# Sixteen weight transfers moved to another engine's queue, and every step ordered anew, in a fused attention and feed-forward kernel

## The chip, the cores and the metric

The kernel runs on one core of a Trainium2 chip. Its time is the device time in microseconds (us) of one execution; of several runs the median is given. Before the change three runs took 532.25, 532.66 and 536.98 us, so the median is 532.66 us.

## The reference: what is computed

Inputs r, k, v, w are (4 batches, 8 heads, 768 positions, 48), u is (8, 48), all as 64-bit floats; w_in is 384 x 2048 and w_out is 2048 x 384. A recurrent attention runs over the positions, and its output goes through a feed-forward stage:

```python
for t in range(S):
    cur = einsum('bhd,bhe->bhde', u * k[t], v[t])
    y[t] = einsum('bhd,bhde->bhe', r[t], state + cur)
    state = w[t][..., None] * state + einsum('bhd,bhe->bhde', k[t], v[t])
x = y.transpose(0, 2, 1, 3).reshape(B * S, H * D)      # 3072 x 384
h = maximum(x @ w_in, 0.0)
out = (h * h) @ w_out
```

## The kernel before, in words

**Tiles.** The 768 positions are cut into 6 chunks of 128. For each chunk and each of the 4 batches (a unit; 24 in all) the attention is done in matrix form, and its result x is written as a high and a low part. When the batches of a chunk have their x, the feed-forward stage takes them: w_in and w_out are held as 8 groups, each of two 128-wide blocks f, so there are 16 steps f for each chunk. A step is nine matmuls into a PSUM bank `hp` (line 852), relu on ScalarE (L857), square (ScalarE L859 in chunk 0, VectorE L861 later), a rounded high part on ScalarE (L863), the rest on VectorE (L864), and then three matmuls for each batch into that batch's bank `ob` (L870). A step takes all four batches (512 columns, "full width") or, by `HALF`, only two (256 columns): the first 6 steps of chunk 0 and all 16 of chunk 1 are done in halves.

**Weights.** The weights arrive as 64-bit numbers. `load_w` fetches a group of w_in by five transfers into `ri` (L398: one to 96 partitions, two to 48 and two to 16) and a group of w_out by one into `ro` (L400), all issued on SP. `split_w` makes high and low parts of each: a widening copy on ScalarE (L411), three integer operations on VectorE (L415, L419, L424), a cast on ScalarE (L431) and a subtraction on GpSimd (L432). The result is `wi` and `wo`, which L852 and L870 read.

**Attention.** In chunk 0 TensorE turns the inputs (L496), VectorE scans the decay (L508), ScalarE and VectorE form its logarithms and quotients (L515 to L535), TensorE forms bonus terms (L548), scores (L736) and outputs (L760, L777, L752, L770). From chunk 1 on the turned inputs `pt` come by transposes on VectorE (L460) and transfers inside SBUF (L470), and the matmuls are L608, L626 (outer products), L653 (scores), L644 (state times r) and L663 (output). Pieces of x are copied between partitions by transfers issued on SP (L705).

**Order.** Every piece of work is a step that `P.add` records with its engine and the steps it depends on. The table `ORDER` then says in which order all 2473 steps are issued; as each engine runs its own instructions in order, the table fixes the queue of every engine. `PLACES` says which buffer of a pool each use gets. `FILLS` puts filler matmuls (L334: transposes of the identity matrix into an unused part of PSUM, no result is read) ahead of some TensorE steps; 16 more run at the start. The steps of `load_w` are made in a loop:

```python
for i, (to, src) in enumerate(pieces):
    n = (2 * R, D, D, D, D)[i]
    P.add("sp", (1.45, 0.72, 0.72, 0.47, 0.47)[i], rank(0), lambda to=to, src=src: nc.sync.dma_start(out=to, in_=src),
          w=[("wi", g, i)], after=before, runs=n, issue=0.48)
```

The functions that the change touches:

Of the kernel before, what the change touches and what calls it, by code (L numbers as in the profile page):

```python
# [96 lines left out]
class Names:  # L97
# [122 lines left out]
def kernel(  # L220
# [11 lines left out]
    nc = tc.nc  # L232
# [3 lines left out]
    DM, DF = w_in.shape  # L236
    C = 128
# [4 lines left out]
    HP = J + D  # L242
# [772 lines left out]
```

## Time and profile before

| | |
|---|---|
| median of three runs | 532.66 us |
| span of the profiled execution | 533.0 us |
| TensorE busy (matmul) | 515.3 us, 97% |
| VectorE busy | 358.4 us, 67% |
| ScalarE busy | 312.6 us, 59% |
| granted TensorE clock, mean | 0.999 |
| filler matmuls | 142, 22.7 us of TensorE's busy time |

The span reaches from the first to the last instruction; no other time of the profiled execution is given, so the span is what the sum is made against. It lies 0.3 us above the median. A busy engine is not one that does useful work: fillers count as busy, and a matmul's end is modelled. Idle time of an engine matters only where another waits for it.

### The profile page before, as it was taken

The page shows a single profiled execution, that of the slowest core. Times are in us where ns is not written, and L with a number is a line of the kernel's source. Part 1 is how long each engine was busy: PE and PEld are TensorE (multiplying, and loading weights), DVE is VectorE, ACT ScalarE, POOL GpSimd, SP SyncE. Part 2 cuts the span into 40 slices and gives each one's busy share as a digit, 9 for nine tenths or more (in the row PEclk, how much of TensorE's full clock was granted, in tenths as well). Part 3 has the DMA queues.
Part 4 walks back from the last instruction along what each step waited for, and adds up shares of the span by engine and source line. Part 5 has one row for each costly group of instructions (what it writes and reads, how often), then busy time and mean ns, then how long its engine had stood idle before and what let it go on. Part 6 is the DMA issues. An engine that isn't in the chain of part 4 may idle for free.

```text
span 533.0 us, 13849 instructions
## 1 busy us (share of the span) xinstructions
PE 515.3 (97%) x5478; PEld 464.7 (87%) x5478; DVE 358.4 (67%) x782; ACT 312.6 (59%) x858; POOL 77.6 (15%) x117
## 2 busy tenths in 40 slices
PE   8998999999999999899999999999999999999996
PEld 8787998778899989788998988898998898989995
DVE  4899887887768799766877768648366654333332
ACT  2778888777675667757557384655345554432322
POOL 2012441242403030030300300201200000000000
PEclk9999999999999999999999999999999999999999
DMA  9999869946465655636555363543450010200001
GB/s 144 168 241 218 179 148 204 236 81 119 85 129 121 117 117 109 124 77 129 107 92 110 61 134 73 100 77 80 89 117 1 5 31 17 71 6 1 0 1 63
DMA packets 222982, 53.07 MB, mean 100 GB/s; under 512 B 212672, under 2 KB 217792, under 8 KB 222912
## 3 DMA queue, kind: packets, MB, share of 16 engines
q1 hardware_dynamic: 222192, 51.15, 48.1%
q8 instruction: 45, 0.74, 0.6%
q10 hardware_dynamic: 720, 0.98, 0.6%
q14 instruction: 25, 0.20, 0.1%
HBM read 31.65 MB, written 4.72 MB: 68 GB/s over the span
## 4 chain that ended last, share of the span: by engine, by line
PE 69%; SPq 3%; DVE 2%; DMA 2%; issue 0%; ACT 0%; POOL 0%; ACTq 0%; DVEq 0%; POOLq 0%
PE ob L870 31%; PE hp L852 30%; SPq L470 2%; PE ob L644 2%; PE ob L663 2%; PE a L653 2%; PE a L626 1%; PE hp L608 1%; DMA x<-x 1%; DVE st L460 0%; DMA pt<-st 0%; DMA v<-in_v_dram 0%; SPq L483 0%; PE hp L548 0%; DVE pt L508 0%
## 5 line engine op out<-in xcount | busy, mean ns | idle before, releaser
L870 PE MATMUL ob<-wo,g 128*128 128x384 f32 x1152 | 228.1, 341 | 2.1 <-ACT x L584 2.1
L852 PE MATMUL hp<-x,wi 128*128 128x512 f32 (+1 forms) x1062 | 220.9, 354 | 1.5 <-DVE g L864 1.3
L870 PEld LDWEIGHTS ob<-wo,g 128*128 128x128 f32 x1152 | 199.6, 188 | 9.6 <-ACT x L584 2.3
L852 PEld LDWEIGHTS hp<-x,wi 128*128 128x128 f32 x1062 | 174.6, 189 | 27.7 <-DVE g L864 4.0
L857 ACT ACTIVATE t<-hp 128x512 f32<-128x512 f32 (+1 forms) x118 | 61.0, 517 | 89.1 <-PE hp L852 53.5
L861 DVE SCALAR_TENSOR_TENSOR hp<-hp,t 128x512 f32<-128x512 f32 (+1 forms) x96 | 58.1, 605 | 78.3 <-ACT t L857 78.1
L864 DVE TENSOR_TENSOR g<-hp,g 128x512 fp32r<-128x512 f32 (+1 forms) x118 | 69.1, 586 | 39.9 <-ACT g L863 38.4
L863 ACT CAST g<-hp 128x512 fp32r<-128x512 f32 (+1 forms) x118 | 59.5, 507 | 47.0 <-DVE hp L861 46.2
L603 ACT ACTIVATE m<-diag,beta 128x64 f32<-128x64 f32 x160 | 40.3, 339 | 0.0
L508 DVE TENSOR_TENSOR_SCAN pt<-pt,zero 112x128 f32<-112x128 f32 x80 | 30.8, 420 | 7.3 <-DMA pt<-st 4.1
L634 POOL MEMSET S<- 1x1 f32 x16 | 1.4, 88 | 193.1 <-PE ob L644 192.5
L584 ACT ACTIVATE x<-ob 112x128 fp32r<-112x128 f32 x64 | 15.7, 277 | 21.0 <-PE ob L663 13.6
L557 POOL TENSOR_TENSOR st<-st 128x384 f32<-128x384 f32 x16 | 16.6, 1035 | 78.3 <-DVE st L460 53.2
L460 DVE STREAM_TRANSPOSE st<-st 128x1152 f32<-128x1152 f32 x20 | 26.9, 1360 | 0.2 <-DMA st<-in_w_dram 0.2
L587 DVE SCALAR_TENSOR_TENSOR x<-ob,x 112x128 fp32r<-112x128 f32 x64 | 16.6, 282 | 13.1 <-ACT x L584 9.3
L432 POOL TENSOR_TENSOR wi<-q,wi 128x768 fp32r<-128x768 f32 x8 | 16.2, 2026 | 50.1 <-ACT wi L431 46.5
L515 ACT ACTIVATE m<-pt 112x512 f32<-112x512 f32 x24 | 15.2, 632 | 9.0 <-DVE pt L508 8.8
L531 DVE TENSOR_TENSOR pt<-pt,m 112x512 f32<-112x512 f32 x24 | 17.2, 716 | 4.3 <-ACT Ec L530 1.9
L801 ACT COPY ob<-zero 112x128 f32<-112x128 f32 x64 | 16.3, 271 | 4.8 <-DVE x L587 3.2
L432 POOL TENSOR_TENSOR wo<-q,wo 128x768 fp32r<-128x768 f32 x8 | 14.8, 1856 | 25.0 <-ACT wo L431 22.7
L610 ACT COPY m<-hp 128x448 f32<-128x448 f32 (+1 forms) x20 | 9.9, 494 | 13.5 <-PE hp L608 13.2
L685 DVE COPY_PREDICATED m<-caus,a 128x256 f32<-128x256 uint8 x40 | 16.9, 439 | 1.1 <-PE a L653 1.0
(127 smaller groups left out, 540.1 us busy)
## 6 DMA issues: line engine op xcount, KB each, us to landing
pt<-st SPq DMA_DIRECT2D x120, 96.0 KB, 2.3
ro<-in_moe_w_out_dram SPq DMA_DIRECT2D x8, 768.0 KB, 6.6
v<-in_v_dram SPq DMA_DIRECT2D x96, 48.0 KB, 2.5
st<-in_r_dram SPq DMA_DIRECT2D x11, 384.0 KB, 5.1
st<-in_w_dram SPq DMA_DIRECT2D x11, 384.0 KB, 5.2
st<-in_k_dram SPq DMA_DIRECT2D x11, 384.0 KB, 4.6
out_dram<-q SPq DMA_DIRECT2D x20, 192.0 KB, 2.2
ri<-in_moe_w_in_dram SPq DMA_DIRECT2D x8, 384.0 KB, 5.2
```

The lines of the kernel that those rows point to most:

```text
L432: P.add("pool", 1.9, rank(8 * k + 5), lambda q=q, tt=tt: G.tensor_tensor(out=tt[:, 1], in0=q.tile, in1=tt[:, 0].bitcast(F32), op=ALU.subtr ...
L460: V.transpose(out=zt[:, i].rearrange("a t p q i -> a t (p q) i"), in_=sv[:, :, i].rearrange("s t p q x -> s t (p q) x"))
L508: lambda p=p: V.tensor_tensor_scan(out=pt[:, 0, p], data0=src(0)[:, p], data1=zero.broadcast_to([HP, C]), initial=1.0, op0=ALU.mult, op1=A ...
L531: P.add("dve", 0.6, rank("kn"), lambda: V.tensor_tensor(out=pt[:, 0], in0=pt[:, 0], in1=yv(), op=ALU.mult), r=[y0], w=EK, port=True)
L603: A.activation(M.tile[:, o:o + Q], diag2, AF.Copy, scale=beta.tile[:, i:i + 1])
L685: P.add("dve", 0.36, rank("mask"), lambda j=j: V.copy_predicated(out=mv(j), mask=caus[:, :, 0:Q].unsqueeze(1).broadcast_to([128, 2, 2, Q]) ...
L852: T.matmul(hp.tile[:, 0:n], wi[f][:, wl, kt], xT[:, kt, xl, xs], start=(m == 0), stop=(m == 3 * KT - 1))
L857: P.add("act", 0.49 if full else 0.28, rank("g1"), lambda: A.activation(t(), h(), AF.Relu), r=[hp], w=[(g, 1)])
L861: P.add("dve", 0.605 if full else 0.337, rank("g2"), lambda: V.scalar_tensor_tensor(out=h(), in0=h(), scalar=0.0, in1=t(), op0=ALU.max, op ...
L863: P.add("act", 0.48 if full else 0.26, rank("g3"), lambda: A.copy(out=hi(), in_=h()), r=[hp], w=[(g, 0)])
L864: P.add("dve", 0.605 if full else 0.335, rank("g4"), lambda: V.tensor_tensor(out=lo(), in0=h(), in1=hi().bitcast(F32), op=ALU.subtract), r ...
L870: T.matmul(obs[b][:, 0:DM], g.tile[0][:, gl, o:o + C], wo[f][:, wl], start=(f == 0 and m == 0), stop=(f == NF - 1 and m == 2))
```

## The change

Three things change in the code. The last two of the five transfers of each w_in group (the ones to 16 partitions, 16 transfers in all) are issued from ScalarE's queue; nothing is changed in what they move. `ORDER`, `PLACES` and `FILLS` are replaced throughout. The step that clears an output half of a PSUM bank (`clear`) gets a dependency on the chunk-0 steps that use this bank. Below, two lines of the tables stand for them.

```diff
 ORDER = (
-    0, 4, 11, 6, 94, 1, 14, 18, 5, 19, 20, 17, 10, 21, 8, 9, 139, 15, 7, 16, 12, 23, 2, 13, 24, 22, 25, 92, 26, 30, 27, 101,
...
+    2468, 2464, 2450, 2469, 2461, 2465, 2466, 2462, 2463, 2471, 2449, 2458, 2472, 2459, 2460,
 )
 FILLS = {
-    443: (2, 'a', 1), 571: (3, 'a', 0), 363: (3, 'a', 0), 370: (4, 'hp', 1), 578: (5, 'hp', 1), 493: (3, 'hp', 0), 645: (2, 'side', 0), 511: (6, 'side', 0),
-    520: (2, 'side', 0), 634: (5, 'side', 0), 663: (4, 'hp', 0), 1215: (1, 'hp', 1), 15: (29, 'ob', 1), 30: (8, 'ob', 3), 39: (6, 'ob', 0), 80: (6, 'ob', 2),
-    89: (5, 'hp', 0), 142: (3, 'hp', 0), 124: (12, 'ob', 0), 133: (11, 'ob', 0), 162: (6, 'ob', 0),
+    55: (4, 'ob', 0), 14: (3, 'ob', 0), 57: (6, 'ob', 1), 56: (6, 'ob', 1), 16: (9, 'ob', 1), 30: (8, 'a', 0), 140: (10, 'ob', 3), 39: (8, 'ob', 1),
+    41: (3, 'ob', 1), 48: (18, 'ob', 2), 100: (2, 'ob', 2), 80: (4, 'hp', 0), 82: (3, 'hp', 0), 89: (7, 'ob', 1), 121: (4, 'ob', 0), 124: (2, 'ob', 0),
+    126: (3, 'ob', 0), 167: (3, 'side', 0),
 }
...
         for i, (to, src) in enumerate(pieces):
             n = (2 * R, D, D, D, D)[i]
-            P.add("sp", (1.45, 0.72, 0.72, 0.47, 0.47)[i], rank(0), lambda to=to, src=src: nc.sync.dma_start(out=to, in_=src),
+            e = nc.sync if i < 3 else nc.scalar
+            P.add("sp" if i < 3 else "actq2", (1.45, 0.72, 0.72, 0.47, 0.47)[i], rank(0), lambda to=to, src=src, e=e: e.dma_start(out=to, in_=src),
                   w=[("wi", g, i)], after=before, runs=n, issue=0.48)
...
         for p in range(NP):
-            P.add("act", 0.16, rank("zero"), lambda p=p: A.copy(out=obs[p][0:HP, DM:], in_=zero[0:HP].broadcast_to([HP, C])), w=[("YO", p)], banks=1 << p)
+            turned = [s for s in P.steps if s.name.endswith(f" of chunk 0, batch {s.name[-1]}") and ("ob", p) in s.keys]
+            P.add("act", 0.16, rank("zero"), lambda p=p: A.copy(out=obs[p][0:HP, DM:], in_=zero[0:HP].broadcast_to([HP, C])), w=[("YO", p)], after=turned, banks=1 << p)
```

**What the order shows.** In the changed kernel, line numbers are 12 to 14 higher. The matmuls on TensorE are the same in number and shape, but for the fillers: 142 before, 119 now. Their places, counted in TensorE's queue between four marks that both orders have:

| stretch of TensorE's queue | fillers before | fillers now | other work that the order moves across the marks |
|---|---|---|---|
| up to the first half-width feed-forward step (L852, 128x256) | 73 | 107 | now also one more group of four L496 and one more of four L548 |
| from there to the first full-width step (group 3 of w_in) | 31 | 12 | that much less, and 57 matmuls L870 instead of 60 |
| from there to the first step of group 7 | 28 | 0 | 84 matmuls L870 instead of 81 |
| from there to the first full-width step of chunk 2 | 10 | 0 | the same |

The fillers of the first stretch include the 16 at the start. ScalarE's queue holds 5 of the 16 moved transfers ahead of the relu of the first half-width step, 8 more ahead of the relu of the first full-width step, and the last 3 behind it. A check of the decay values (one matmul, a comparison on VectorE and a read of the flag by every engine) moves from 472 us (L914) to the last steps of the program. Ahead of the latter relu it also holds one more cast of w_in, one of w_out (L431), one L578 and one L801 than before.

First place: TensorE's queue at the first half-width feed-forward step. `x_136` is x of chunk 0, `wi_57` group 0 of w_in, `st_138` raw inputs of batches 2 and 3, `ident` the identity. Before:

```order
L334 MATMUL hp_145<-ident 128x128 x3
L496 MATMUL a_147<-ident,st_138 128x128 x4
L852 MATMUL hp_146<-x_136,wi_57 128x256 x9
L548 MATMUL ob_141<-ut,m_161 128x4 x4
L496 MATMUL ob_143<-ident,st_138 128x128 x4
L852 MATMUL hp_145<-x_136,wi_57 128x256 x9
```

Now:

```order
L509 MATMUL ob_143<-ident,st_138 128x128 x4
L509 MATMUL a_148<-ident,st_138 128x128 x4
L866 MATMUL hp_145<-x_136,wi_57 128x256 x9
L866 MATMUL hp_146<-x_136,wi_57 128x256 x9
L346 MATMUL ob_141<-ident 128x128 x4
```

The bonus matmuls (L548) and the last turned inputs (L496) stood behind the first step and stand ahead of it now; the two blocks of group 0 follow each other.

Second place: ScalarE's queue between two widening copies of w_in and w_out (L411 before, L424 now). Before:

```order
L431 CAST wo_59<-q_150 128x768
L411 ACTIVATE q_149<-ri_60 128x768
L781 COPY ly_89<-a_147 112x128
L554 COPY beta_173<-ob_144 64x2x2x2 x2
L411 ACTIVATE q_150<-ro_62 128x768
L859 ACTIVATE hp_145<-t_96 128x256
```

Now, with `ri_60` group 1 and `ri_64` group 2 of raw w_in:

```order
L411 DMA ri_64<-in_moe_w_in_dram 16x3x512
L794 COPY ly_90<-a_147 112x128
L411 DMA ri_60<-in_moe_w_in_dram 16x3x512
L591 ACTIVATE st_137,far<-st_137,nfar 128x8x48
L529 ACTIVATE m_156<-m_156 112x512
L444 CAST wi_57<-q_150 128x768
L597 ACTIVATE x_136<-a_147 128x128
L597 ACTIVATE x_136<-a_148 128x2x128
L798 COPY m_158<-a_147 128x224
L798 COPY m_158<-a_148 128x224
L424 ACTIVATE q_149<-ri_60 128x768
```

The queue that evacuates PSUM now issues transfers too, and the copy that reads group 1 stands seven instructions behind the issue of that group's last piece. For group 2 there are six instructions between the two.

Third place: TensorE's queue in the first unit of chunk 1, between its outer products, its scores and the product with the state. Before:

```order
L626 MATMUL a_148<-v_153,m_158 48x48
L334 MATMUL hp_146<-ident 128x128 x4
L653 MATMUL a_147<-pt_129 64x64 x2
...
L334 MATMUL hp_146<-ident 128x128 x5
L644 MATMUL a_148<-pt_129,S_131 64x64
```

Now:

```order
L866 MATMUL hp_146<-x_136,wi_73 128x512 x9
L561 MATMUL hp_145<-ut,m_159 128x4 x4
L666 MATMUL a_147<-pt_129 64x64 x2
...
L884 MATMUL ob_141<-wo_75,g_99 128x384 x3
L884 MATMUL ob_144<-wo_71,g_97 128x384 x3
L884 MATMUL ob_144<-wo_75,g_99 128x384 x3
L884 MATMUL ob_142<-wo_71,g_97 128x384 x3
L657 MATMUL a_148<-pt_129,S_131 64x64
```

Where four and five fillers stood between the attention's steps, nine matmuls of a full-width step and twelve matmuls L870 (L884 now) stand.

## Rows read from the trace of the kernel before

**Rows 1.** Busy time, share of the span and instructions of each engine, from the page.

```profile
PE 515.3 (97%) x5478; PEld 464.7 (87%) x5478; DVE 358.4 (67%) x782; ACT 312.6 (59%) x858; POOL 77.6 (15%) x117
```

**Rows 2.** Busy time of each engine in six stretches, granted clock, DMA share, GB/s.

```profile
0.00:33.00 33.00, 28.98 (x361) 25.72 (x362) 22.99 (x62) 17.70 (x52) 4.40 (x21) 1.00 1.01 173
33.00:74.37 41.37, 39.17 (x434) 36.30 (x433) 36.18 (x58) 34.51 (x88) 13.41 (x8) 1.00 0.86 201
74.37:121.17 46.80, 44.60 (x462) 37.55 (x462) 40.69 (x69) 37.19 (x88) 15.51 (x10) 1.00 0.78 166
121.17:231.53 110.36, 106.04 (x1440) 98.84 (x1440) 86.94 (x226) 76.83 (x250) 18.33 (x27) 1.00 0.59 113
231.53:528.41 296.88, 296.52 (x2787) 266.30 (x2786) 171.09 (x371) 146.32 (x384) 25.92 (x53) 1.00 0.31 62
528.41:533.00 4.59, 0.00 (x0) 0.00 (x0) 0.56 (x1) 0.00 (x0) 0.00 (x0) 0.87 0.28 98
```

**Rows 3.** The same view for the fillers (L334) alone: PE and PEld busy.

```profile
0.00:33.00 33.00, 12.37 (x73) 10.97 (x73) 1.00 1.01 173
33.00:74.37 41.37, 4.21 (x31) 3.39 (x31) 1.00 0.86 201
74.37:121.17 46.80, 4.53 (x28) 3.32 (x28) 1.00 0.78 166
121.17:231.53 110.36, 1.63 (x10) 1.17 (x10) 1.00 0.59 113
```

**Rows 4.** PE in order of time: start, duration, idle before and its releaser.

```profile
1.60 3.68 PE L334 MATMUL a<-ident 128*128 128x128 f32 x16 [1.60 <-POOL ident masks.py:199]
32.59 0.66 PE L496 MATMUL a<-ident,st 128*128 128x128 f32 x4 [0.33 <-DVE S L792]
33.00 1.39 PE L852 MATMUL hp<-x,wi 128*128 128x256 f32 x9
34.23 0.95 PE L548 MATMUL ob<-ut,m 112*128 112x4 f32 x8
74.37 2.24 PE L852 MATMUL hp<-x,wi 128*128 128x512 f32 x9
121.17 2.24 PE L852 MATMUL hp<-x,wi 128*128 128x512 f32 x9
125.21 1.05 PE L548 MATMUL hp<-ut,m 112*128 112x4 f32 x8 [0.73 <-DVE m L523]
218.74 0.79 PE L870 MATMUL ob<-wo,g 128*128 128x384 f32 x3 [2.08 <-ACT x L584]
```

**Rows 5.** ScalarE's busy time between its first and later marks.

```profile
8.56:76.71 68.15, 52.71 (x142) 1.00 0.92 193
```

**Rows 6.** ScalarE in order of time: the marks, and its cast and far instructions.

```profile
8.56 0.63 ACT L515 ACTIVATE m<-pt 112x512 f32<-112x512 f32 x1 [5.96 <-DVE pt L508]
76.71 0.59 ACT L857 ACTIVATE t<-hp 128x512 f32<-128x512 f32 x1
77.19 0.83 ACT L431 CAST wi<-q 128x768 fp32r<-128x768 f32 x1
75.59 0.62 ACT L578 ACTIVATE st<-st,nfar 128x384 f32<-128x384 f32 x1
76.11 0.19 ACT L578 ACTIVATION_READ_ACCUMULATOR st<-st,nfar 128x1 f32 x1
219.00 0.28 ACT L801 COPY ob<-zero 112x128 f32<-112x128 f32 x1
```

**Rows 7.** Issues of transfers: duration min/median/max, and time to landing.

```profile
L398 SPq DMA_DIRECT2D ri<-in_moe_w_in_dram x40: 317/590/2796, 15.8 to 99.4; - x40
DMA to landing us min/median/max: 2.4/4.9/7.6
L372 ACTq DMA_DIRECT2D un<-in_u_dram x1: 429/429/429, 0.8 to 0.8; - x1
```

**Rows 8.** The chain of waits, in order of time, around 214 us and at the end.

```profile
214.61 3.57 DMA x<-x
218.41 0.29 ACT x L584
521.52 6.87 PE ob L870 x39
528.41 0.56 DVE m L877
```

190 rows, old and new, of tables (ORDER, PLACES) are left out of this document.

## The prediction, as it was put on record before the changed kernel ran

> **What bounds the kernel now.** I read the engines' busy line first, then the same by stretches, then the fillers, then the two queues that the change touches. TensorE is busy 97% of the span, VectorE 67%, ScalarE 59% [rows 1]. The windows cut the span at five marks of TensorE's queue: the first half-width step (33.00 us), the first full-width one (74.37), the first of group 7 (121.17), the first full-width one of chunk 2 (231.53) and TensorE's end (528.41) [rows 2, 4]. I call the stretches A to E, and the rest the tail. TensorE is idle 4.02, 2.20, 2.20, 4.32 and 0.36 us in A to E (length less busy time), and the tail takes 4.59: 17.7 us in all. The granted clock is 1.00 in A to E, the higher of its two levels, so the sum has no term for the clock.
>
> Busy is not useful: 12.37, 4.21, 4.53 and 1.63 us of A to D are fillers [rows 3]. Useful work is thus 16.61, 34.96, 40.07 and 104.41 us. Idle time and fillers of A to D are 35.5 us, and this is all that an order can win there; E has nothing to give. How much of it is won hangs on whether the inputs are ready when TensorE has nothing but useful work left. In A and B VectorE is 70% and 87%, ScalarE 54% and 83% busy, and the transfer engines 1.01 and 0.86 [rows 2]: much stands close behind TensorE.
>
> **The change, part by part.**
>
> *Stretch A.* The marks move: one group of four turns (L496, 0.66 us) and one group of four bonus matmuls (half of the 0.95 us row, but I count all of it: A may be 0.5 too long by that and B too short, the sum of both is the same) stand ahead of the first half-width step now [rows 4]. Useful: 16.61 + 0.66 + 0.95 = 18.22. Fillers: 107 instead of 73. The first 16 take 3.68 us [rows 4]; the other 57 took 12.37 − 3.68 = 8.69, or 0.152 each, so 91 take 13.87, and all 107 take 17.55. Idle as before, 4.02. A = 39.8 instead of 33.0.
>
> *Stretch B.* Useful: 34.96 − 1.61 (moved to A) − 0.53 (three L870 moved to C, at 6.87/39 = 0.176 each [rows 8]) = 32.82. Twelve fillers at 4.21/31 = 0.136 are 1.63. Idle 2.20 as before. To this comes a wait that the trace of before can't have: ScalarE now issues the last pieces of groups 1 and 2 shortly before its own copy reads them, and TensorE, VectorE and the next steps are queued behind that copy. Such a transfer took 2.4 us at best, 4.9 in the median, 7.6 at most from issue to landing [rows 7]. For group 1 the instructions between take about 0.81 + 0.63 + 0.83 + 2 x 0.29 + 2 x 0.28 = 3.4 us, an estimate from like instructions [rows 6, 8]; six smaller ones stand between for group 2, some 2 us. The wait is therefore 0 at a landing of 2.4 (0.4 at group 2), 1.5 + 2.9 = 4.4 at 4.9. I take 1.0, nearer to the low end: these pieces are the smallest of the five and are alone in ScalarE's queue, while the median is of transfers that stand behind others on SP. Against it, the Trainium skill ("DMA: Bandwidth & Descriptors", "Queues, rings and completion order") says that each transfer engine takes turns between its queues, a packet at a time; by that a second queue is served early and the wait would be 0 to 0.4. No row here shows two busy queues side by side. B = 32.82 + 1.63 + 2.20 + 1.0 = 37.7 instead of 41.4.
>
> A + B = 77.4 against 74.4: **+3.1**. From below, if no wait is left but the 1.60 us ahead of the first filler [rows 4]: 18.22 + 32.82 + 17.55 + 1.63 + 1.60 = 71.8, or −2.6. From above it is ScalarE that decides. Between 8.56 and its first full-width relu at 76.71 it worked 52.71 us and stood idle 15.44 [rows 5, 6]. Now it has 2.74 more to do in that stretch (two casts at 0.83, one L578 at 0.81, one L801 at 0.28 [rows 6]) and 13 issues. An issue took ScalarE 0.43 us the one time it made one; on SP the median is 0.59 [rows 7]. At 0.43 the 13 are 5.6 us. If all its idle time stayed, it would be 2.74 + 5.6 = 8.3 us late; if its idle time takes the new work up, it is 61.1 us busy of about 71, 86% instead of 77%, and adds nothing. I take the second for the sum, because TensorE's own queue is 3 us longer there and gives ScalarE that time.
>
> *What SP gains.* Sixteen issues at 0.59 are 9.4 us less on SP [rows 7]. I cost that at nothing: in A the transfer engines are busy throughout (1.01 [rows 2]), so an earlier issue only waits in another place. The Trainium skill says the same more strongly ("DMA: Bandwidth & Descriptors", "Issuing engines are not separate DMA queues"): all issuers end at the same 16 engines, and only the short time of issuing is saved. If SP's issuing set the landings instead, up to 13 x 0.59 = 7.7 us would be saved in A and B; TensorE's own work would let 2.6 of that through.
>
> *Stretch C.* Useful 40.07 + 0.53 = 40.60, no fillers instead of 28, idle 2.20 as before: 42.8 instead of 46.8, **−4.0**. This counts all 28 fillers as time won, that is, that useful matmuls stand where they stood and are ready. Bounds: −6.2 if the idle time goes too; +0.5 if all the fillers' time comes back as waiting.
>
> *Stretch D.* Useful 104.41, no fillers instead of 10 (1.63 us). Of the idle time the 0.73 us ahead of L548 goes, since a full-width step stands ahead of it now. The 2.08 us ahead of L870 stays: it is a transfer of x (3.57 us, then 0.29 of ScalarE [rows 4, 8]), still issued on SP among others. D = 104.41 + 4.32 − 0.73 = 108.0 instead of 110.4: **−2.4**, with −6.0 and 0 for bounds.
>
> *Stretch E and the tail.* The same work in nearly the same order and 0.36 us idle: 0. The check that moves to the end waits on one matmul and one small VectorE instruction, and its reads run beside the last output transfer of the 4.59 us tail [rows 2]; the last copy to SBUF (0.56 [rows 8]) is of the same size for another batch. 0, at most 0.5 either way. The new dependency of `clear` costs nothing, since the chunk-0 steps that it names are long past when its turn comes; the work behind which it hides is all of C.
>
> *Sum:* +3.1 − 4.0 − 2.4 = −3.3; span 533.0 − 3.3 = 529.7. The span stands 0.3 above the median of the runs, so the forecast is **529.4 us**.
>
> **The rivals.**
>
> 1. *The early stage goes faster, too.* The fillers in A stand where TensorE would wait anyway, and the fitted order halves the idle time. A idle 1.60 + 1.21 = 2.81, B 1.10 without the new wait: A + B = 18.22 + 17.55 + 2.81 + 32.82 + 1.63 + 1.10 = 74.1 (−0.2); C −5.1; D −1.63 − 2.16 = −3.8. Sum −9.1: 523.6 us. For it: SP is freed, and the order is made for the real arrival times. Against it: in A there are more fillers than before, which says that more waiting is expected there, not less.
>
> 2. *The fillers' time comes back as waiting.* A filler costs nothing where TensorE would have waited. If half of what C and D save (2.3 + 0.8 us) comes back, the sum is −0.2; if all, +3.5 with D's 0.73 still won: 532.5 to 536.2 us. For it: VectorE is 87% busy in B and C, so that it may be what C waits for [rows 2].
>
> 3. *ScalarE becomes the bound of A and B: slower.* Its 15.44 us of idle time are waits for VectorE's and TensorE's results in the same chain, and stay. Each issue costs 0.59, as on SP. First full-width relu at 8.56 + 15.44 + 52.71 + 2.74 + 13 x 0.59 = 87.1 instead of 76.7: +10.4. With C and D as forecast (−6.4) this is +4.0, 536.7 us; with three of the issues at the 2.80 us of the longest on SP, 543. It decides once A and B lose more than 6.4, which at 0.59 an issue is when 11.4 or more of the 15.44 idle us can't be used. Against it: 86% is not full.
>
> That the change doesn't do what it says is no case of its own: the transfers are as many and as large, and what the order does is rival 1 or 2.
>
> **How the numbers follow.** Forecast 0.40 (its own range 526.5 to 532.3), rival 1 0.20, rival 2 0.25, rival 3 0.15. One per cent, about what a measurement can tell from no change, is 5.3 us: below 527.3 is faster, above 538.0 slower. Faster: all of rival 1 and 0.13 of the forecast's lower part, 0.33. Slower: the upper half of rival 3 and a little for a mishap in it, 0.12. Within: 0.55. All low bounds together are −14.8 (518 us); I take the range from 520.5, since they won't all meet, to 537.5, which leaves out the upper part of rival 3: some 0.05 below and 0.13 above.
>
> **What would show it.** In the profile of the changed kernel, by TensorE's queue: the first half-width step near 39.8 us, the first full-width near 77.4, group 7 near 120.2, chunk 2 near 228.2; 119 fillers of about 19 us; transfers on ScalarE of 0.4 to 0.6 us each; ScalarE some 86% busy from its first instruction to the first full-width relu. A first full-width step ahead of 75 is rival 1; idle time in C of 4 us or more is rival 2; a first full-width relu behind 84 us with ScalarE's idle time near 15 is rival 3. The forecast is wrong from its root if the first half-width step comes at 33 or earlier with 107 fillers ahead of it: then fillers stand for waiting, and A can't be summed from them.

## The result, and the profile after

The changed kernel is **slower**: 542.12 us (median of 4 runs, 538.21 to 544.54) against 533.42 (4 runs), a ratio of 1.0128 with a 95% interval of 1.0081 to 1.0176; run again later, 1.0152 (1.0105 to 1.0198). Ratios, here and below, leave out the slow runs, those over 1.5 per cent above the fastest of their kernel, while the times are medians of all runs. The forecast was 529.4 us, with 537.5 as the range's upper end. The profiled execution took 544.54 us, 2 us more than its span of 542.5; the prediction had taken a span of 533.0 us to stand 0.3 us above the median of the times.

The engines' busy line of the page, which answers to [rows 1]: TensorE's share fell to 95%, though it does the same useful work.

```profile
PE 516.9 (95%) x5455; PEld 467.0 (86%) x5455; DVE 360.2 (66%) x782; ACT 311.2 (57%) x858; POOL 77.1 (14%) x117
```

The changed kernel by the same five marks; it answers to [rows 2], with the same columns:

```profile
0.00:45.16 45.16, 34.54 (x407) 31.14 (x408) 28.48 (x70) 22.90 (x65) 8.15 (x23) 0.92 0.98 181
45.16:81.66 36.50, 36.38 (x400) 33.60 (x398) 29.04 (x51) 29.91 (x79) 11.40 (x6) 0.95 0.68 158
81.66:128.61 46.95, 42.72 (x437) 36.14 (x438) 41.41 (x65) 36.93 (x88) 12.89 (x7) 0.96 0.72 163
128.61:239.16 110.55, 106.12 (x1431) 99.73 (x1430) 88.87 (x229) 74.54 (x246) 19.50 (x30) 0.98 0.59 115
239.16:537.04 297.88, 297.10 (x2786) 266.34 (x2786) 172.41 (x370) 146.42 (x384) 25.14 (x52) 1.00 0.31 62
537.04:542.50 5.46, 0.01 (x1) 0.00 (x0) 0.00 (x0) 0.48 (x1) 0.00 (x0) 0.84 0.25 83
```

The fillers alone in the first two (there are none in the next two); it answers to [rows 3]:

```profile
0.00:45.16 45.16, 16.63 (x107) 14.26 (x107) 0.92 0.98 181
45.16:81.66 36.50, 2.42 (x12) 1.71 (x12) 0.95 0.68 158
```

| stretch | before | forecast | now |
|---|---|---|---|
| A, to the first half-width step | 33.00 | 39.8 | 45.16 |
| B, to the first full-width step | 41.37 | 37.7 | 36.50 |
| C, to group 7 | 46.80 | 42.8 | 46.95 |
| D, to chunk 2 | 110.36 | 108.0 | 110.55 |
| E | 296.88 | 296.88 | 297.88 |
| tail | 4.59 | 4.59 | 5.46 |

A is 5.4 us longer than forecast, C 4.1, D 2.5, E and the tail 1.9 together; B is 1.2 shorter. TensorE's idle time in A is 45.16 − 34.54 = 10.6 us (4.0 before), and its granted clock, 1.00 before, is below that in A to D.

Where A goes: ScalarE's queue from 18 us on (start, duration, engine, line and operation; in brackets the idle time before and what ended it; ACTq rows are issues of transfers):

```profile
18.68 0.60 ACT L590 ACTIVATE st<-st,nmid 128x384 f32<-128x384 f32 x1
25.27 0.32 ACTq L411 DMA_DIRECT2D ri<-in_moe_w_in_dram  x1
25.69 0.27 ACT L794 COPY ly<-a 112x128 f32<-112x128 f32 x1 [6.40 <-DMA st<-in_k_dram]
26.05 0.33 ACTq L411 DMA_DIRECT2D ri<-in_moe_w_in_dram  x1
```

and TensorE's around it:

```profile
20.56 0.55 PE L346 MATMUL ob<-ident 128*128 128x128 f32 x3
26.10 1.62 PE L790 MATMUL a<-ly,sel 112*128 112x128 f32 x6 [5.00 <-ACT ly L794]
```

A transfer of w_in that should go out at 19.28 goes out at 25.27. The 6.40 us end with the landing of another transfer, one of k that SP issued. The copy of `ly` behind it needs nothing of either, but it stands in the same queue; TensorE waits 5.00 us for it. That transfer of k, with its time from issue to landing in us as the last number:

```profile
18.04 0.45 SPq L464 DMA_DIRECT2D st<-in_k_dram  x1
```

```profile
st<-in_k_dram SPq DMA_DIRECT2D x1, 384.0 KB, 7.2
```

So it landed at 25.2 us. What the two transfers have to do with each other the built program says (engine's rows with the counters that each waits for; first ScalarE, then SP):

```
L590 ACTIVATE st00_137<-st00_137,nmid_122 128x8x48 [waits DMAHW1_49]
L411 DMA ri1_60<-in_moe_w_in_dram 16x3x512 [waits DMAHW1_49]
L794 COPY ly0_89<-a1_148 112x128 [waits DVE_49,PE_49]

L411 DMA ri0_56<-in_moe_w_in_dram 96x2x512 [waits DMAHW0_49]
L464 DMA st01_138<-in_k_dram 128x16x48 [waits DMAHW1_49]
L496 DMA v01_92<-in_v_dram 64x4x48 [waits DMAHW3_49]
```

In this program the transfers of SP and ScalarE share eight landing counters (DMAHW0 to 7) and take them in turn. From the ninth on, an issue waits until the transfer that last used its counter has landed, unless its queue has waited for that landing already. Here both transfers have DMAHW1: ScalarE's issue starts at 25.27 us, when k has landed. While it waits, ScalarE evacuates no PSUM.

### The profile page after: what moved, and what is told of

Read it like the earlier page. It is cut to its first block, busy times and chain, and to the rows that moved or that the text cites. A ratio compares the mean times of both kernels' runs of the same rounds, so it can differ in the third digit from the quotient of the medians.

```text
span 542.5 us, 13794 instructions
## 1 busy us (share of the span) xinstructions
PE 516.9 (95%) x5455; PEld 467.0 (86%) x5455; DVE 360.2 (66%) x782; ACT 311.2 (57%) x858; POOL 77.1 (14%) x117
## 4 chain that ended last, share of the span: by engine, by line
PE 69%; SPq 10%; DVE 8%; DMA 5%; ACT 4%; issue 2%; POOL 0%; DVEq 0%; ACTq 0%; POOLq 0%
PE ob L884 30%; PE hp L866 30%; SPq L483 4%; SPq L496 3%; DVE st L473 2%; SPq L464 2%; PE ob L657 2%; PE ob L676 1%; PE a L666 1%; DMA ro<-in_moe_w_out_dram 1%; DMA ri<-in_moe_w_in_dram 1%; DMA v<-in_v_dram 1%; PE a L639 1%; SPq L411 1%; DMA pt<-st 1%
## 5 line engine op out<-in xcount | busy, mean ns | idle before, releaser
L884 PE MATMUL ob<-wo,g 128*128 128x384 f32 x1152 | 229.6, 342 | 2.0 <-DVE pt L544 1.1
L866 PE MATMUL hp<-x,wi 128*128 128x512 f32 (+1 forms) x1062 | 223.9, 357 | 2.0 <-DVE g L878 1.4
L884 PEld LDWEIGHTS ob<-wo,g 128*128 128x128 f32 x1152 | 201.4, 189 | 9.7 <-DVE g L878 1.5
L866 PEld LDWEIGHTS hp<-x,wi 128*128 128x128 f32 x1062 | 176.6, 191 | 28.2 <-DVE g L878 2.9
L544 DVE TENSOR_TENSOR pt<-pt,m 112x512 f32<-112x512 f32 x24 | 18.6, 775 | 3.6 <-ACT m L529 3.1
L545 DVE SCALAR_TENSOR_TENSOR m<-pt,m 112x512 f32<-112x512 f32 x24 | 16.4, 685 | 0.4
```

What stands on the lines that cost most here:

```text
L544: P.add("dve", 0.6, rank("kn"), lambda: V.tensor_tensor(out=pt[:, 0], in0=pt[:, 0], in1=yv(), op=ALU.mult), r=[y0], w=EK, port=True)
L866: T.matmul(hp.tile[:, 0:n], wi[f][:, wl, kt], xT[:, kt, xl, xs], start=(m == 0), stop=(m == 3 * KT - 1))
L884: T.matmul(obs[b][:, 0:DM], g.tile[0][:, gl, o:o + C], wo[f][:, wl], start=(f == 0 and m == 0), stop=(f == NF - 1 and m == 2))
```

## The experiments

Ratios are to the kernel before on the same chip, whose median was 533.7 to 536.1 us there; 5 rounds each. In this table only the order and the issuer of the 16 transfers differ:

| 16 transfers issued on | old order | new order |
|---|---|---|
| SP | 1 | 1.0226 (1.0168 to 1.0283) |
| ScalarE | 1.0267 (1.0211 to 1.0324) | 1.0128 and 1.0152 |
| GpSimd | 1.0085 (1.0045 to 1.0125) | 1.0018 (0.9981 to 1.0054) and 1.0026 |

**new_sp**

```diff
-            e = nc.sync if i < 3 else nc.scalar
+            e = nc.sync
```

> The changed kernel with all its 16 moved transfers issued on SP again; order, buffers and fillers stay. Theory W (a transfer's issue on ScalarE waits until an earlier transfer has landed, and everything behind it in ScalarE's queue waits too): the 6.4 us stop of ScalarE at 19 to 25 us and TensorE's 5.0 us wait at 21 us go, and with them the stretch of half clock behind; first half-width step at 36 to 40 us, time 530 to 536 us. Rival O (the new order with fewer fillers is what costs): the same waits and low clock at other places, 538 to 543 us.

547.6 us, above what either theory gave. A is 44.75 us. ScalarE does not stop at an issue any more, but a little later and in another form. Its row, TensorE's and SP's:

```profile
31.35 0.89 ACT L424 ACTIVATE q<-ri 128x768 f32<-128x768 f32 x1 [6.68 <-DMA ri<-in_moe_w_in_dram]
```

```profile
34.05 0.90 PE L773 MATMUL a<-m,v 64*48 64x128 f32 x8 [6.17 <-DVE S L805]
```

```profile
19.92 5.73 SPq L496 DMA_DIRECT2D v<-in_v_dram  x4
25.70 3.66 SPq L411 DMA_DIRECT2D ri<-in_moe_w_in_dram  x7
```

On SP the last pieces of group 0 queue behind four v transfers that take 5.73 us to issue, and the copy that the new order has ScalarE do at 24.7 us waits 6.68 us for them. VectorE's queue stands behind that copy, and TensorE waits 6.17 us for VectorE. So the new order needs these pieces out of SP's queue: within it, ScalarE is the better issuer of the two (1.0226 against 1.0128 and 1.0152; the intervals overlap at their ends), and theory W as written (put them back and the loss is gone) fell. What is left of it is that a stop in ScalarE's queue, by issue or by data, costs TensorE about its length.

**old_act** (of the line, the part that changes)

```diff
-lambda to=to, src=src: nc.sync.dma_start(out=to, in_=src)
+lambda to=to, src=src, e=nc.sync if i < 3 else nc.scalar: e.dma_start(out=to, in_=src)
```

> The kernel before with one edit: the same 16 transfers issued on ScalarE, at the places that the old order gives them. Theory W: ScalarE stops at some of them for several us ahead of the first half-width step, TensorE waits, 538 to 548 us. Rival O: the queue costs nothing, 531 to 535 us.

549.5 us: theory W, and a little more. The stop is here, too, and TensorE waits 8.0 us for the `ly` behind it:

```profile
25.85 0.63 ACT L577 ACTIVATE st<-st,nmid 128x384 f32<-128x384 f32 x1
34.13 0.32 ACTq L398 DMA_DIRECT2D ri<-in_moe_w_in_dram  x1
34.57 0.89 ACT L411 ACTIVATE q<-ri 128x768 f32<-128x768 f32 x1 [8.09 <-DMA v<-in_v_dram]
```

**new_pool** and, beside the last experiment, **new_pool_again**: the changed kernel with `nc.gpsimd` in place of `nc.scalar`.

> The changed kernel with the 16 transfers issued on GpSimd, which is idle from 4 to 32 us. Theory W: the waits at the issue stop nobody, ScalarE runs on; 529 to 536 us, like or below the version on SP. Rival O: 538 to 543 us.

536.57 and 536.14 us, as theory W said. GpSimd's issues took 0.5 to 0.8 us each, the first five were out by 10.1 us, and none of them waited long. In the built program the transfers of GpSimd have counters of their own (DMASW0 to 7), so the edit does two things: ScalarE issues none of the 16, and these no longer share counters with SP's transfers. In the changed kernel SP stood at two issues of `pt` until w_in transfers of ScalarE's on the same counters had landed (us in total, times, longest):

```profile
SPq L483 <- DMA ri<-in_moe_w_in_dram: 8.4, 2, 5.2
```

With GpSimd that wait is not there; what it cost is not shown by itself. A, B and C in the second profile:

```profile
0.00:36.82 36.82, 32.56 (x407) 29.58 (x408) 28.14 (x70) 22.89 (x65) 11.79 (x29) 1.00 1.06 182
36.82:75.25 38.43, 36.06 (x400) 32.36 (x398) 29.89 (x51) 29.74 (x79) 17.03 (x15) 1.00 0.96 187
75.25:120.22 44.97, 42.64 (x436) 36.22 (x437) 41.19 (x65) 36.77 (x88) 12.86 (x8) 0.96 0.83 173
```

The stop at 19 us is gone. Having the 16 on ScalarE, with the shared counters, thus costs the changed kernel 1.0 to 1.3 points of its 1.3 to 1.5; the order with its free issuer is no faster than the kernel before.

**old_pool**: the same edit in the old order.

> The kernel before with the same 16 transfers on GpSimd, order untouched. Theory W (who stops at an issue decides, not the transfers): within 1 per cent of the kernel before, 531 to 537 us; a gain of some us if SP's 16 freed issues bring other transfers earlier. Rival (the moved transfers take the transfer engines' time from the first inputs, whoever issues them): 538 us or more.

540.16 us, 1.0085: the rival. In the profile, of a run of 542.37 us, A is 37.59 us, and TensorE waited in it for raw k:

```profile
15.02 1.97 PE L496 MATMUL ob<-ident,st 128*128 128x128 f32 x8 [5.56 <-DMA st<-in_k_dram]
```

GpSimd had issued five pieces of weights between 3.4 and 6.2 us, while SP was still issuing the first inputs. With the pieces of groups 0 to 2 left on SP (old_pool_late below) A is 33.32 us, as before. A free issuer is not a free transfer.

**new_3pool**: of the 16, only the three that stand ahead of 32 us on ScalarE go to GpSimd.

```diff
+            e = nc.sync if i < 3 else nc.gpsimd if (g, i) in ((0, 3), (0, 4), (1, 3)) else nc.scalar
```

> The changed kernel with three of the 16 transfers on GpSimd: those ahead of 32 us in ScalarE's queue, at one of which ScalarE stood 6.4 us. The other 13 stay on ScalarE. Theory S (this one stop is nearly all that the queue costs): 535 to 538 us, like the kernel with all 16 on GpSimd (536.6). Rival (the 13 later issues stop ScalarE as well): 539 to 543 us, near the changed kernel.

541.42 us, 1.0122 (1.0076 to 1.0169): theory S fell. The stop moved to the second of the issues that are left on ScalarE:

```profile
31.03 0.27 ACT L794 COPY ly<-a 112x128 f32<-112x128 f32 x1 [0.23 <-PE a L773]
36.94 0.36 ACTq L411 DMA_DIRECT2D ri<-in_moe_w_in_dram  x1
37.35 0.61 ACT L591 ACTIVATE st<-st,nfar 128x384 f32<-128x384 f32 x1 [6.06 <-DMA ro<-in_moe_w_out_dram]
```

**new_6pool**: groups 0 to 2 on GpSimd, groups 3 to 7 on ScalarE (`nc.gpsimd if g < 3 else nc.scalar`).

> The changed kernel with the six transfers of groups 0 to 2 on GpSimd and the ten of groups 3 to 7 on ScalarE. Theory E (ScalarE stops at whichever issue meets the crowded transfers up to some 45 us; later ones cost little): 535 to 538 us, as with all 16 on GpSimd. Rival (the later ones cost as well): 539 to 543 us.

538.27 us, 1.0051 (1.0026 to 1.0076): theory E. The six early transfers make up most of the loss; the longest wait at one of the ten later issues is 2.4 us.

**old_act_late** and **old_pool_late**: the old order with the ten transfers of groups 3 to 7 on ScalarE, or on GpSimd.

> The kernel before with only the ten transfers of groups 3 to 7 on ScalarE, six stay on SP. Theory E: little is lost, 533 to 538 us, against the 549.5 with all 16 there. Rival (every issue there costs its share): 10/16 of 14.6, 541 to 546 us.

> The kernel before with the ten transfers of groups 3 to 7 on GpSimd, whose queue holds them behind its first work at 30 us or later; six stay on SP. If the loss of the version with all 16 there (540.2) came from weights fetched ahead of the first inputs, it is gone: 531 to 536 us, and the version that may beat the kernel before by up to 3 us. Otherwise 538 to 542.

541.44 us, 1.0115 (1.0073 to 1.0157), and 538.69 us, 1.0035 (1.0005 to 1.0065). The first time lies in the rival's range, but not by its path: no issue stopped ScalarE for long, and A and B are 33.67 and 41.39 us, as before; yet C is 53.04. The shared counters work the other way round, too: here an issue of SP (`pt`) waited for a transfer of ScalarE's. SP's wait (us in total, times, longest), and the issue on ScalarE that it was for by the program's counters:

```profile
SPq L470 <- DMA ri<-in_moe_w_in_dram: 6.6, 1, 6.6
```

```profile
70.32 0.32 ACTq L398 DMA_DIRECT2D ri<-in_moe_w_in_dram  x1
```

SP's issue before it ended at 68.7 us; this one went out at 75.35, when ScalarE's transfer had landed. From there SP's queue is late: three transfers of `pt` that it issued from 76.00 us before, it issues from 81.03 us. VectorE waited for `pt`, TensorE 2.06 us for VectorE, and then ran at the lower of its two levels. VectorE's row, TensorE's, and windows of TensorE's next 15 us:

```profile
84.91 0.42 DVE L508 TENSOR_TENSOR_SCAN pt<-pt,zero 112x128 f32<-112x128 f32 x1 [1.86 <-DMA pt<-st]
```

```profile
85.98 1.86 PE L548 MATMUL hp<-ut,m 112*128 112x4 f32 x8 [2.06 <-DVE m L523]
```

```profile
80.00:90.00 10.00, 7.94 (x36) 7.18 (x36) 5.64 (x12) 6.33 (x14) 3.22 (x2) 0.80 0.70 122
90.00:95.00 5.00, 5.00 (x16) 4.23 (x17) 3.21 (x6) 3.16 (x11) 0.00 (x0) 0.50 1.14 202
```

TensorE's busy time in C is 49.17 us against 44.60 for the same work. Neither theory had this path; that the half clock makes C longer here was seen, not tested. The version with GpSimd loses little and wins nothing: A is 33.32 us, as its theory said, but C is 49.71, and why was not tested.

**old_nofill_late** and **old_nofill**: the old order without its 38 fillers in C and D (entries of `FILLS` taken out), and without all 126 that `FILLS` places.

> The kernel before without its 38 fillers between the first full-width step and chunk 2 (6.2 us of TensorE's time). Theory F (they stand where TensorE waits anyway): no change within 2 us, 533 to 536 us. The forecast's step (their time is won): 528 to 530 us. A third way (without them the clock falls): 536 to 540 us.

> The kernel before without all its 126 placed fillers (19 us; the 16 at the start stay). Theory F: no gain; the waits show instead, and the half clock behind them costs some us: 535 to 545 us. If the fillers cost their time, 515 to 525 us.

535.32 us, 1.0007 (0.9977 to 1.0037), and 543.16 us, 1.0165 (1.0102 to 1.0227): theory F both times. C and D without their 6.2 us of fillers:

```profile
74.45:121.69 47.24, 42.42 (x435) 35.61 (x435) 40.70 (x69) 37.10 (x88) 15.52 (x10) 0.96 0.78 164
121.69:229.55 107.86, 104.27 (x1431) 97.98 (x1430) 86.97 (x226) 76.85 (x250) 18.34 (x27) 1.00 0.59 114
```

C is 0.4 us longer without 28 fillers: the longest waits of TensorE there end with VectorE (1.9 us in two, for `g`). D is 2.5 shorter in this profile, but seven profiles of the old order have D between 107.7 and 111.1 with much the same work in it, so one D tells little. Without all 126, stretch B is:

```profile
37.95:85.20 47.25, 42.66 (x403) 40.12 (x402) 36.48 (x58) 34.20 (x87) 13.10 (x8) 0.82 0.75 161
```

It is 5.9 us longer than before, and TensorE is busy 42.66 us with 34.96 us of useful work [rows 2, 3], at a granted clock of 0.82. Here the lower level may well have cost time; it was not tested apart from the waits.

**new_fill**: `41: (36, 'ob', 1)` in place of `41: (3, 'ob', 1)`, that is, 33 more fillers in the 5.00 us wait.

> The changed kernel with 36 fillers instead of 3 ahead of the sixth-matmul group (L790) that waited 5.0 us. They fill the wait and shorten nothing, so they show the clock's part: if the half clock after 24 us is what the idle TensorE brought on, it stays at 1.00 there and the time falls by 2 to 4 us (538 to 540); if the clock falls for another reason, no change (541 to 543).

542.15 us, 1.0123 (1.0082 to 1.0164). The clock did what was expected, the time did not. The changed kernel, then this one:

```profile
26.00:32.00 6.00, 5.90 (x44) 5.54 (x45) 3.00 (x6) 3.53 (x9) 0.00 (x0) 0.50 0.99 232
```

```profile
26.00:32.00 6.00, 5.33 (x87) 4.87 (x88) 3.14 (x6) 3.03 (x9) 0.00 (x0) 1.00 0.89 197
```

With full clock TensorE did the work of this window sooner and then waited for VectorE (2.26 us at 42 us, 1.2 in the changed kernel), with a granted clock of 0.89 from 32 us on where it was 0.99; A is 45.23 against 45.16 us. The half clock behind the stop is real and costs A nothing that these runs can show, since TensorE is not what A waits for.

**new_pool_fill**: the 16 on GpSimd, as in new_pool, and 25 fillers at three waits in C (added at the end of `FILLS`).

```diff
+    455: (6, 'side', 0), 358: (10, 'side', 0), 365: (9, 'side', 0),
```

> The changed kernel with all 16 transfers on GpSimd and 25 fillers (some 3.5 us) put back at three places between the first full-width step and group 7, where TensorE waited 0.9, 1.5 and 1.5 us and then ran at half clock. Theory K (there the half clock binds: it follows the waits and lengthens the steps that set the time): clock 1.00 in that stretch, 1 to 3 us less than without them, 533 to 535.5 us. Rival (the stretch waits for VectorE and the transfers, whatever the clock): no change or up to 2 us more, 536 to 539 us.

> The same without those fillers, beside it on this chip: 0.998 to 1.006 of the kernel before, by every theory.

536.34 against 536.14 us. In C the clock is 1.00 instead of 0.96, and C is 44.97 us in both:

```profile
76.40:121.37 44.97, 43.69 (x462) 37.62 (x462) 41.03 (x65) 37.32 (x88) 12.86 (x8) 1.00 0.82 174
```

So the rival: in the new order C is as long at either clock. The waits of TensorE in C that are left (1.3 us the longest) end with VectorE in both profiles; that C waits for transfers, too, is not shown.

**new_again**: the changed kernel unedited.

> The changed kernel once more, beside the others on this chip, for a narrower interval: 1.008 to 1.018 of the kernel before, 538 to 544 us, by every theory.

543.13 us, 1.0152; the stop before `ly` was 7.3 us in its profile.

No version was faster than the kernel before.

## Why the prediction was wrong, step by step

- **The price of an issue on ScalarE: the step that failed most.** I took 0.43 us from `un`, the first transfer that ScalarE issues, and let ScalarE's idle time take all of it up. The issue itself is even cheaper. What counts is the wait ahead of it, 6.40 us at one issue; the forecast had no term for it, and A came out 5.4 us longer. `un` has no such wait, since its counter was fresh. All 16, and the landing:

```profile
L411 ACTq DMA_DIRECT2D ri<-in_moe_w_in_dram x16: 317/318/833, 15.8 to 111.5; - x16
...
DMA to landing us min/median/max: 2.4/3.3/6.8
```

  The trace of before has such waits in SP's queue, but they are short there, 1.2 us at most in A and B:

```profile
SPq L398 <- DMA ro<-in_moe_w_out_dram: 1.2, 1, 1.2
```

  The length of an issue on SP, 2.80 us at most in [rows 7], is something else. In the changed kernel an issue of k, among the first eight transfers and so with a fresh counter, took 2.51 us:

```profile
2.87 2.51 SPq L464 DMA_DIRECT2D st<-in_k_dram  x1
```

  What makes these issues long is open. The bound from above was the time to landing, 4.9 us in the median and 7.6 at most for w_in in [rows 7], for one issue; rival 3 priced 13 issues at 0.59 each and named 2.80 as the worst. Its number came true, but by luck: it put the first full-width relu at 87.1 us with ScalarE's idle time still 15.44, and the relu came at 87.23 with 24.2 us idle since 8.82.
- **The wait of ScalarE's copies for the transfers just issued (1.0 us in B).** The copy of group 1 waited 2.17 us, in A, and the copy of group 2 not at all. The rule of the Trainium skill cited there ("DMA: Bandwidth & Descriptors", "Queues, rings and completion order"), by which a second queue would be served early, is not borne out by this trace: up to 40 us ScalarE's five pieces took 5.3 us to land in the median, and SP's six pieces of the same size, issued at other times, 3.6:

```profile
ri<-in_moe_w_in_dram SPq DMA_DIRECT2D x6, 96.0 KB, 3.6
ri<-in_moe_w_in_dram ACTq DMA_DIRECT2D x5, 96.0 KB, 5.3
```

- **A = 39.8.** Without the stop it is near, and 2 to 3 us too long: 36.82 and 37.99 us in new_pool_again and new_pool_fill, 37.16 in new_6pool (39.15 in new_pool's profile, of a run of 540.46 us).
- **C, −4.0: wrong.** It counted fillers as time won. Taking them out of the old order won nothing (1.0007), and C in the changed kernel is idle 4.23 us where 2.20 was forecast, and busy 42.72 us with 40.60 of useful work, at a clock of 0.96. With all 16 on GpSimd it is 44.97 us, −1.8 (46.99 in new_pool's profile). Rival 2 had this mechanism, and its sign, 4 us or more of idle time in C. Its upper end was summed wrongly: +3.1 + 0.5 − 0.7 is +2.9, not +3.5.
- **D, −2.4: not shown.** 110.55 us; 107.98 to 109.66 in the versions with GpSimd, within what D does from profile to profile.
- **No clock term.** The clock fell to the lower of its two levels after the stop (0.50 from 26 to 32 us). In A and C of the new order it cost nothing that could be measured, by two experiments; for the longer C of old_act_late and B of old_nofill this is open.
- **SP's freed issues at nothing.** In the old order the freed SP did not make up for anything (1.0085 with GpSimd). In the new order it is the other way: the pieces on SP cost 0.7 to 1 points more than on ScalarE (1.0226 against 1.0128 and 1.0152), since that order reads them earlier than SP can issue them.
- **E and the tail at nothing.** E is about 1 us longer in all profiles of the new order (297.6 to 298.7 against 296.7 to 297.2); the cause is open. The tail is 5.3 to 6.0 us there and 4.6 to 6.2 in the old order, so it is not put down to the moved check.

What stays open: which part of the new order, other than its need for early pieces of group 0, keeps it from being faster with a free issuer. A is 4 to 6 us longer and B 1 to 3 shorter than before there, and A to D together are 228.2, 229.9 and 235.2 us in three profiles, of runs of 533.36, 535.64 and 540.46 us, against 231.5. In the two shorter ones A to D is 1.6 to 3.3 us shorter than before; E takes back about 1, and the median of the runs is no better.

## What to carry to other kernels

A transfer's price on the engine that issues it need not be the issue; it can be the wait for an earlier landing, of another queue's transfer, too. See in the built program which landing each issue waits for, price the wait by the time to landing, and don't let it stand in a queue that others wait for. Where the transfers are crowded, moving an issue can move the stop and not the loss: with three of them moved away a later one stopped ScalarE for about as long, and only with six was most of the loss gone. Fillers cost nothing where the engine waits anyway, so their time must not be counted as won before they are taken out once to see; the same held for the lower clock in the two stretches where it was tested.

## What was not expected of the hardware

The granted clock fell to 0.50 after a wait of 5.00 us in the changed kernel, and after one of 2.06 us in old_act_late, where the same work then took 4.6 us longer. And the same order differs by several us from run to run (538.2 to 544.5). The stop before `ly` was 6.40 us in one profile and 7.3 in another; whether such waits make the difference is not shown.
